# Score banks in two halves, an order for TensorE from a list scheduler, and the causal mask moved to GpSimd, in a two-stage attention kernel

## The chip, the cores and the metric

One core of one Trainium2 chip runs the kernel. The metric is the time of one execution in device microseconds; of a set of runs the median counts. The core has TensorE (PE; its loads of stationary operands are the row PEld), VectorE (DVE), ScalarE (ACT), GpSimd (POOL) and SyncE (SP), each working through its own instructions in order. The queues of DMA transfers that SP and GpSimd start run beside them. PSUM, into which TensorE writes, has eight banks of 512 f32 values for each of the 128 partitions.

## The reference

Two stages follow one another. Stage A is an attention over 8 batches of 12 heads, 448 positions and head size 64; stage B runs four attention experts over its result, of which each token uses two.

```
# stage A, for each batch and head
scores = cap * tanh(q @ k.T / 8 / cap);  attn = softmax(scores);  x[:, head] = attn @ v
# stage B, for each batch; x is 448 x 768
logits = x @ w_gate;  w = softmax over the two largest of four
for e in range(4):
    q, k, v = x @ wq[e], x @ wk[e], x @ wv[e]            # 448 x 64 each
    a = softmax(where(causal, -1e9, q @ k.T / 8));  out += w[e] * (a @ v @ wo[e])
```

The tanh keeps the scores within 30, so that stage A needs no maximum; each score is passed once through Tanh and once through Exp on ScalarE.

## The kernel before

Two heads make a pair: six pairs to a batch, 48 in all. The loop over `p` runs through the pairs, and stage B of a batch is spread over the eight passes behind its last pair, so that both stages share the engines. The order on every engine is the order in which the code issues the work (`manual_schedule`); a table, `batch_b`, says which unit of stage B is issued at which place of which pass.

A pair goes through these steps. `load` fetches the f32 inputs of a whole batch with seven DMAs from SP (the first batch in four groups). `a_cast` (GpSimd) makes f16 copies. `a_tr` (TensorE, then DVE) transposes q and k. `fill0` writes the transposed scores of head 0 and the tails of both heads, four blocks of 128 keys by 448 queries, into a tile of four PSUM banks, and `fill1` the three blocks of head 1. This tile, `ps_score`, exists once: a fill can only start when ScalarE has read the tile's last content, and ScalarE can only go on with scores when the fill is done. `tanh` reads a whole tile (1792 or 1344 values for each partition), `expo` makes the exponentials from its f16 result. `a_pv` multiplies by v, with a column of ones that gives the sum, into two more banks; `a_norm` divides. `a_xt` transposes back into `xT`, and its copy on DVE (L281) also brings the queries, which are held as c·112+p for query 4p+c, into their order with a strided write.

Stage B reads `xT`: `b_v`, `b_gate`, `b_q` and `b_k` project; `b_fill` writes the scores of two experts into the same four-bank tile, a mask being added to each diagonal block by a matmul of `ltm` (L383); `b_exp` takes the exponential of all 1984 columns at once; `b_pv1`, `b_ot` and `b_wo` finish, and the result leaves by DMA from SP. These units use two PSUM banks in turn, `ps_aux`. One pass issues

```
tanh(p,0)  fill1(p)  expo(p-1,1)  a_pv(p-1,0)  a_tr(p+2)  a_cast(p+3)  units of B  tanh(p,1)
fill0(p+1)  expo(p,0)  a_pv(p-1,1)  a_norm(p-1)  units of B  a_xt(p-1)
```

and in two passes of a batch `b_fill` and `b_exp` take the tile between `tanh(p,1)` and `fill0(p+1)`, with `expo(p,0)` cut in two around them.

## Time and profile before

| | |
|---|---|
| Median of 3 runs | 443.25 us (442.03 to 443.75) |
| Profiled execution | 441.75 us, of which its span on the engines 440.0 us |
| Busy: PE, PEld, DVE, ACT, POOL | 311.9, 205.7, 276.6, 305.7, 132.8 us |
| First tanh starts, last expo of stage A ends | 11.66 us, 401.65 us |
| Mean granted clock of TensorE | 0.939 of 2.4 GHz |
| HBM read and written | 36.19 MB, 11.01 MB |

Busy time is the union of an engine's instructions. Two that follow one another closely overlap in the records, so the step from one start to the next is what a chain costs. A busy TensorE is not one at its peak, since a matmul's record also holds the time in which it drains.

### The profile page before, as it was taken

The page shows a single profiled execution, that of the slowest core. Times are in us where ns is not written, and L with a number is a line of the kernel's source. Part 1 is how long each engine was busy: PE and PEld are TensorE (multiplying, and loading weights), DVE is VectorE, ACT ScalarE, POOL GpSimd, SP SyncE. Part 2 cuts the span into 40 slices and gives each one's busy share as a digit, 9 for nine tenths or more (in the row PEclk, how much of TensorE's full clock was granted, in tenths as well). Part 3 has the DMA queues.
Part 4 walks back from the last instruction along what each step waited for, and adds up shares of the span by engine and source line. Part 5 has one row for each costly group of instructions (what it writes and reads, how often), then busy time and mean ns, then how long its engine had stood idle before and what let it go on. Part 6 is the DMA issues. An engine that isn't in the chain of part 4 may idle for free.

```text
span 440.0 us, 8813 instructions
## 1 busy us (share of the span) xinstructions
PE 311.9 (71%) x3568; PEld 205.7 (47%) x3568; DVE 276.6 (63%) x693; ACT 305.7 (69%) x231; POOL 132.8 (30%) x374
## 2 busy tenths in 40 slices
PE   2676686857759677667868587686776678686865
PEld 1354464545535454444536454355544455354442
DVE  6145476567836588468755678365884687557745
ACT  1779797987757777788758877578767887584030
POOL 6793973233223323223322332233232220000000
PEclk9999899899977999999997999779999999979896
DMA  5999998001191012900184012910110001000303
GB/s 139 282 238 229 247 266 253 2 2 72 59 324 51 1 73 80 336 17 37 74 251 144 1 73 65 332 35 2 72 55 3 1 36 72 19 1 9 118 1 125
DMA packets 63497, 46.19 MB, mean 105 GB/s; under 512 B 24288, under 2 KB 59872, under 8 KB 63456
## 3 DMA queue, kind: packets, MB, share of 16 engines
q1 hardware_dynamic: 52944, 44.05, 34.3%
q0 software_dynamic: 10512, 1.58, 4.8%
q8 instruction: 28, 0.46, 0.5%
q14 instruction: 13, 0.11, 0.1%
HBM read 36.19 MB, written 11.01 MB: 107 GB/s over the span
## 4 chain that ended last, share of the span: by engine, by line
PE 45%; DVE 29%; ACT 10%; SPq 6%; issue 5%; DMA 3%; POOL 1%; DVEq 0%; ACTq 0%; POOLq 0%
PE pv L245 8%; PE s L191 6%; ACT pB L389 6%; DVE ob L443 5%; PE kps L357 4%; PE s L202 4%; DVE xT L281 4%; DVE xk L257 4%; PE vps L300 3%; PE sB L378 3%; PE qps L347 3%; PE xtp L270 2%; PE wops L438 2%; DVE kzB L361 2%; DVE kz L180 2%
## 5 line engine op out<-in xcount | busy, mean ns | idle before, releaser
L215 ACT ACTIVATE y<-s 128x1792 f16<-128x1792 f32 x96 | 141.8, 1477 | 53.6 <-PE s L195 33.5
L226 ACT ACTIVATE p<-y 128x1792 f16<-128x1792 f16 (+2 forms) x110 | 147.2, 1339 | 0.0
L136 POOL CAST q<-qf 112x512 f16<-112x512 f32 x48 | 29.5, 614 | 205.1 <-PE tps L164 176.8
L245 PEld LDWEIGHTS <-p 128*128 128x128 f16 x1536 | 66.6, 103 | 21.8 <-issue 6.2
L245 PE MATMUL pv<-v,p 128*128 128x65 f16 x1152 | 66.2, 201 | 0.8 <-ACT p L226 0.8
L281 DVE COPY xT<-xtp 128x448 f16<-128x448 f16 x48 | 55.9, 1164 | 11.4 <-PE xtp L270 11.1
L389 ACT ACTIVATE pB<-sB 128x1984 f16<-128x1984 f32 x16 | 29.2, 1824 | 46.2 <-PE sB L383 46.2
L191 PE MATMUL s<-qt,kz 128*128 128x448 f16 x144 | 40.7, 397 | 27.1 <-ACT pB L389 24.9
L245 PE MATMUL pv<-vtz,p 128*128 128x65 f16 x384 | 58.8, 199 | 0.0
L255 DVE RECIPROCAL rc<-pv 128x8 f32<-128x8 f32 x48 | 10.0, 208 | 75.6 <-PE pv L245 75.6
L438 PE MATMUL wops<-wo,oT 128*128 128x384 f16 x128 | 32.2, 348 | 18.2 <-DVE kz L180 10.3
L177 DVE COPY qt<-tps 128x576 f16<-128x576 f16 x48 | 22.3, 465 | 33.8 <-PE tps L171 33.7
L202 PE MATMUL s<-qt,kz 128*128 128x448 f16 x144 | 39.7, 389 | 4.9 <-ACT y L215 4.8
L443 DVE COPY ob<-wops 128x384 f32<-128x384 f32 (+1 forms) x64 | 34.6, 557 | 5.6 <-PE wops L438 4.6
L257 DVE TENSOR_TENSOR xk<-pv,rc 128x512 f16<-128x512 f32 x48 | 33.2, 692 | 1.7
L270 PE MATMUL xtp<-ident,xk 128*128 128x128 f16 x144 | 17.2, 232 | 23.4 <-DVE xk L257 20.6
L191 PEld LDWEIGHTS <-kz 128*128 128x128 f16 x144 | 14.7, 106 | 38.8 <-issue 32.9
L164 PE MATMUL tps<-ident,q 112*128 112x112 f16 x192 | 19.1, 227 | 13.2 <-POOL q L136 9.3
L270 PEld LDWEIGHTS <-xk 128*128 128x128 f16 x192 | 12.6, 102 | 33.9 <-DVE xk L257 25.9
L347 PE MATMUL qps<-xT,wq 128*128 128x448 f16 x96 | 23.3, 384 | 5.9 <-DVE ob L443 5.8
L300 PE MATMUL vps<-wvg,xT 128*128 128x260 f16 x192 | 26.5, 283 | 1.0
L146 POOL CAST v<-vf 128x384 f16<-128x384 f32 x48 | 24.4, 507 | 8.9 <-DMA vf<-in_v_dram 6.2
(86 smaller groups left out, 510.9 us busy)
## 6 DMA issues: line engine op xcount, KB each, us to landing
qf<-in_q_dram SPq DMA_DIRECT2D x7, 1344.0 KB, 8.5
out_dram<-ob SPq DMA_DIRECT2D x24, 384.0 KB, 2.3
kf<-in_k_dram SPq DMA_DIRECT2D x7, 1152.0 KB, 10.8
vf<-in_v_dram SPq DMA_DIRECT2D x7, 1152.0 KB, 8.3
out_dram<-ob SPq DMA_DIRECT2D x8, 192.0 KB, 2.7
ktf<-in_k_dram SPq DMA_DIRECT2D x14, 96.0 KB, 9.4
vtf<-in_v_dram SPq DMA_DIRECT2D x14, 96.0 KB, 6.8
qf<-in_q_dram SPq DMA_DIRECT2D x2, 448.0 KB, 5.1
```

Source lines behind the costliest of these rows:

```text
L191: nc.tensor.matmul(sc[:, c, 0:S], kk[:, 0, 128 * c : 128 * (c + 1)], qt[:, 0:S], start=True, stop=True,)
L202: nc.tensor.matmul(sc[:, c, 0:S], kk[:, 1, 128 * c : 128 * (c + 1)], qt[:, 0:S], start=True, stop=True,)
L215: nc.scalar.activation(yt, sc[:, 0:n, 0:S], AF.Tanh, scale=isc / capf)
L226: nc.scalar.activation(pt[:, c0:c1, :], yt[:, c0:c1, :], AF.Exp, scale=capf)
L245: nc.tensor.matmul(pv[:, g, 65 * n : 65 * n + 65], lhsT, rhs, start=(c == 0), stop=(c == KC),)
L257: nc.vector.tensor_tensor(xk.rearrange("p n g d -> p g n d"), pv[:, :, :, 0:64], rc.broadcast_to((128, 2, 4, Dh)), ALU.mult,)
L270: nc.tensor.transpose(ps[:, 128 * n : 128 * (n + 1)], src(n), ident if n < 3 else swap)
L281: nc.vector.tensor_copy(xT[b][:, j, :].rearrange("m (p c) -> m c p", c=QC), ps[:, 0:S].rearrange("m (c p) -> m c p", c=QC),)
L300: nc.tensor.matmul(ps, xT[b][:, j, WIN[n] : WIN[n] + 128], wvg[:, j, :], start=(j == 0), stop=(j == NDC - 1))
L389: nc.scalar.activation(pb[:, 64:2048], s.pop(("sc", r))[:, 0:1984], AF.Exp, scale=isc)
L438: nc.tensor.matmul(ps, s["oT"][r][:, w : w + 128], wo2[r][:, f * (D // 2) : (f + 1) * (D // 2)], start=(r == 0), stop=(r == 1),)
L443: nc.vector.tensor_copy(ob[lo:128, f * (D // 2) : (f + 1) * (D // 2)], ps[lo:128, :])
```

## The change

The score tile becomes two tiles of two banks each. A pair's seven blocks go through them in four parts (`HALF`: 2, 2, 2 and 1 blocks), each part with a `fill` and a `tanh` of its own, and the two tiles are refilled in turn: while ScalarE reads one, TensorE may write the other. `expo` stays one instruction for four and one for three blocks. Stage B's scores go the same way, one expert (1024 or 960 columns) for each half tile. ScalarE's order is written down as a list, `prog`: for each pair two tanhs, the exponential of the head before, two tanhs, the exponential of head 0, with stage B's exponentials (`X`) in two passes of a batch.

TensorE's order is no longer a table. A class `Plan` keeps estimated clocks of TensorE, DVE and ScalarE while the program is built. Before each fill it issues the units that can start before the half tile comes free (`pump`), and holds back those that would end too late for the fill; it forces what the fill depends on. Stage B's units of a batch carry earliest times spread over 36 us. Nothing of this runs on the chip; it only sets the order of the instructions.

The causal mask is taken off TensorE: instead of adding -30000 before the exponential, GpSimd sets the masked values to zero after it, with eight `affine_select`s for each two experts. The fills read the queries in another order, with a strided moving operand, as a block of 384 columns and one of 64, so that each window of 128 columns holds 128 successive queries; the transposes of `a_xt` then bring them into order by a permuted identity, and the copy to `xT` becomes contiguous. `a_pv` has a bank of its own for each head and divides at once, so that reciprocal and product come once for each head; there are four auxiliary banks for it and all other units. Loads come pair by pair, seven ahead; casts run four ahead. Before the first transposes fourteen matmuls on zeros are issued, and pair 0 is cast by DVE.

```diff
+class Plan:
...
+    LAT = 0.2
...
+    def emit(self, u):
+        start = max(self.pe, self.ready(u))
+        u["fn"]()
+        self.pe = start + u["pe"]
+        end = self.pe + self.LAT
+        if u["dve"]:
+            self.dve = max(self.dve, end) + u["dve"]
+            end = self.dve + self.LAT
+        if u["aux"]:
+            self.aux[self.naux % 4] = end
+            self.naux += 1
+        self.done[u["key"]] = end
...
+    def pump(self, until, latest):
+        while self.pe < until and (self.work or self.paced):
+            best = None
+            for q in (self.work, self.paced[:1]):
+                for u in q:
+                    r = self.ready(u)
+                    if r is not None and (best is None or max(r, self.pe) < best[0]):
+                        best = (max(r, self.pe), u)
+            if best is None or best[0] > until or best[0] + best[1]["pe"] > latest:
+                return
+            u = best[1]
+            (self.work if u in self.work else self.paced).remove(u)
+            self.emit(u)
...
-    stage = ctx.enter_context(tc.tile_pool(name="stage", bufs=2))
+    stage = ctx.enter_context(tc.tile_pool(name="stage", bufs=8))
...
+    def load(p):
...
+        nc.sync.dma_start(qf, q[b, h0:h1].rearrange("h (p c) d -> p h (c d)", c=QC))
+        nc.sync.dma_start(kf, k[b, h0:h1, 0:KM].rearrange("h (p c) d -> p h (c d)", c=KC))
...
+        staged[p] = (qf, kf, vf, ktf, vtf)
...
+    LOAD, CAST, TR = 7, 4, 2
+    for p in range(4):
+        load(p)
...
+    HALF = (((0, 0), (0, 1)), ((0, 2), (0, 3)), ((1, 0), (1, 1)), ((1, 2),))
...
+    def fill(p, i):
...
+        sc = ps_score.tile([128, 2, 512], f32, name=f"s{i}_{p}", tag="score")
+        m = qt[:, 0:S].rearrange("m (c p) -> m c p", c=QC)
+        main = m[:, :, 0:96].rearrange("m c (n t) -> m n c t", t=32)
+        tail = m[:, :, 96:QP]
+        for o, (g, c) in enumerate(HALF[i]):
+            lhsT = qt[:, S : S + 128] if c == KC else kk[:, g, 128 * c : 128 * (c + 1)]
             nc.tensor.matmul(
-                sc[:, c, 0:S], kk[:, 0, 128 * c : 128 * (c + 1)], qt[:, 0:S],
-                start=True, stop=True,
-            )
-        nc.tensor.matmul(sc[:, 3, 0:S], qt[:, S : S + 128], qt[:, 0:S], start=True, stop=True)
-        score[(p, 0)] = sc
-    def fill1(p):
-        qt, kk = qkt.pop(p)
-        sc = ps_score.tile([128, 4, 512], f32, name=f"s1_{p}", tag="score")
-        for c in range(KC):
+                sc[:, o, 0:KM].rearrange("m (n c t) -> m n c t", n=3, c=QC),
+                lhsT, main, start=True, stop=True,
+            )
             nc.tensor.matmul(
-                sc[:, c, 0:S], kk[:, 1, 128 * c : 128 * (c + 1)], qt[:, 0:S],
-                start=True, stop=True,
-            )
-        score[(p, 1)] = sc
+                sc[:, o, KM:S].rearrange("m (c t) -> m c t", c=QC),
+                lhsT, tail, start=True, stop=True,
+            )
+        score[(p, i)] = sc
...
+    def tanh(p, i):
+        g = i // 2
+        n = len(HALF[i])
+        if i % 2 == 0:
+            y[(p, g)] = actp.tile([128, 4 - g, S], f16, name=f"y{g}_{p}", tag=f"y{g}")
+        nc.scalar.activation(
+            y[(p, g)][:, 2 * (i % 2) : 2 * (i % 2) + n, :], score.pop((p, i))[:, 0:n, 0:S],
+            AF.Tanh, scale=isc / capf,
+        )
+    def expo(p, g):
+        pt = actp.tile([128, 4 - g, S], f16, name=f"p{g}_{p}", tag=f"p{g}")
+        nc.scalar.activation(pt, y.pop((p, g)), AF.Exp, scale=capf)
+        pr[(p, g)] = pt
...
+        pv = ps_aux.tile([128, 4, Dh + 1], f32, name=f"pv{g}_{p}", tag="aux")
...
+                nc.tensor.matmul(pv[:, n, :], lhsT, rhs, start=(c == 0), stop=(c == KC))
...
+        nc.vector.reciprocal(rc, pv[:, :, Dh : Dh + 1])
         nc.vector.tensor_tensor(
-            xk.rearrange("p n g d -> p g n d"),
-            pv[:, :, :, 0:64],
-            rc.broadcast_to((128, 2, 4, Dh)),
-            ALU.mult,
+            xt[p][:, :, g, :], pv[:, :, 0:Dh], rc.broadcast_to((128, 4, Dh)), ALU.mult
         )
-        xt[p] = xk
...
-        transpose4(ps, lambda n: xk[:, n, :, :].rearrange("p g d -> p (g d)"))
-        nc.vector.tensor_copy(
-            xT[b][:, j, :].rearrange("m (p c) -> m c p", c=QC),
-            ps[:, 0:S].rearrange("m (c p) -> m c p", c=QC),
-        )
+        transpose4(ps, lambda n: xk[:, n, :, :].rearrange("p g d -> p (g d)"), perm, pswap)
+        nc.vector.tensor_copy(xT[b][:, j, :], ps[:, 0:S])
...
+    def b_fill(b, r, g):
...
+        sc = ps_score.tile([128, 1024], f32, name=f"sB{g}_{b}_{r}", tag="score")
+        if g == 0:
+            nc.tensor.matmul(sc[:, 0:64], kk[:, KM : KM + 128], qe[:, KM:S], start=True, stop=True)
+        for (e, c), o in COL.items():
+            if e == g:
+                n = S - 128 * c
+                o -= 1024 * g
+                ko = e * (S + TL) + 128 * c
+                nc.tensor.matmul(
+                    sc[:, o : o + n], kk[:, ko : ko + 128], qe[:, 128 * c : S],
+                    start=True, stop=True,
+                )
+        s["sc", r, g] = sc
...
+    def b_exp(b, r, g):
...
+        pb = pB[2 * (b % 2) + r]
+        n = 1024 - 64 * g
+        o0 = 64 + 1024 * g
+        nc.scalar.activation(
+            pb[:, o0 : o0 + n], st[b].pop(("sc", r, g))[:, 0:n], AF.Exp, scale=isc
         )
+        blocks = [(o, 0, 128, 128) for (e, _), o in COL.items() if e == g]
+        if g == 0:
+            blocks += [(0, 0, 64, 64), (0, 64, 128, 64)]
+        for o, r0, r1, n in blocks:
+            blk = pb[r0:r1, 64 + o : 64 + o + n]
+            nc.gpsimd.affine_select(
+                out=blk, in_=blk, compare_op=ALU.is_ge, fill=0.0, base=0,
+                pattern=[[1, n]], channel_multiplier=-1,
+            )
...
+    dummy = ps_aux.tile([128, 512], f32, name="dummy", tag="aux")
+    for _ in range(14):
+        nc.tensor.matmul(dummy, warm[:, 0:128], warm, start=True, stop=True)
...
+    a_cast(0, nc.vector)
+    a_tr(0)
     a_cast(1)
...
+    nc.vector.tensor_copy(
+        perm.rearrange("r (p c) -> r c p", c=QC), ident.rearrange("r (c p) -> r c p", c=QC)
+    )
...
+    prog = []
+    for p in range(NP + HP):
+        ops = []
+        if p < NP:
+            ops += [("S", p), ("T", p, 0), ("T", p, 1)]
+        else:
+            ops += [("S", p)]
+        xb = EXPB.get(p)
+        if xb:
+            ops.append(("X", *xb, 0))
+        if 1 <= p <= NP:
+            ops.append(("E", p - 1, 1))
+        if xb:
+            ops.append(("X", *xb, 1))
+        if p < NP:
+            ops += [("T", p, 2), ("T", p, 3), ("E", p, 0)]
+        prog += ops
...
+    def do_fill():
+        nonlocal nfill
+        o = reads[nfill]
+        rel = ends[nfill - 2] if nfill >= 2 else 0.0
+        cost = 0.43 if o[0] == "X" else 0.38 if o[2] < 3 else 0.19
+        dep = fill_dep(o)
+        plan.force(dep)
+        at = plan.act + sum(dur(x) for x in prog[pos : where[nfill]])
+        plan.pump(rel, at - cost - 0.4)
+        plan.pe = max(plan.pe, rel, plan.done[dep]) + cost
+        fill(*o[1:]) if o[0] == "T" else b_fill(*o[1:])
...
+    def slot(p):
+        load(p + LOAD)
+        if CAST <= p + CAST < NP:
+            a_cast(p + CAST)
+            plan.done[("cast", p + CAST)] = plan.act + 4.0
+        if p < 4:
+            weights(p)
+        if p + TR < NP:
+            plan.add(work, ("tr", p + TR), 0.43, 0.95, [("cast", p + TR)], a_tr, p + TR)
+        if p >= 1 and p <= NP:
+            plan.add(work, ("pv", p - 1, 0), 0.73, 0.55, [("E", p - 1, 0)], a_pv, p - 1, 0)
+            plan.add(
+                work, ("pv", p - 1, 1), 0.73, 0.55, [("E", p - 1, 1), ("pv", p - 1, 0)],
+                a_pv, p - 1, 1,
+            )
+            plan.add(work, ("xt", p - 1), 0.22, 0.35, [("pv", p - 1, 1)], a_xt, p - 1)
+        if p >= HP and p % HP == 0:
+            batch(p // HP - 1)
...
+    def batch(b):
...
+        for r in range(2):
+            plan.add(u, ("q", b, r), 1.13, 0.55, [x], b_q, b, r)
+            plan.add(u, ("k", b, r), 1.13, 0.75, [x], b_k, b, r)
+            for n in range(2 * r, 2 * r + 2):
+                plan.add(u, ("v", b, n), 0.66, 0.6, [x], b_v, b, n)
+        plan.add(u, ("g", b), 0.0, 1.4, [("v", b, 3)], b_gates, b, aux=False)
+        for e in range(E):
+            plan.add(
+                u, ("pvB", b, e), 0.46, 0.7, [("X", b, e // 2, e % 2), ("g", b)], b_pv, b, e
+            )
+            if e % 2:
+                plan.add(u, ("oT", b, e // 2), 0.22, 0.35, [("pvB", b, e)], b_ot, b, e // 2)
+        for n in range(4):
+            for f in range(2):
+                plan.add(u, ("wo", b, n, f), 0.33, 0.5, [("oT", b, 1)], b_wo, b, n, f)
+        if b < B - 1:
+            for i, t in enumerate(u):
+                t["nb"] = plan.act + 4.0 + i * 36.0 / len(u)
+        paced.extend(u)
```

## Rows read from the trace of the kernel before

**Rows 1.** Waits, by who waited for whom: total us, times, longest us.
```profile
ACT pB L389 <- PE sB L383: 46.2, 16, 5.7
...
ACT y L215 <- PE s L195: 33.5, 34, 9.6
...
ACT y L215 <- PE s L202: 19.8, 20, 1.4
```

**Rows 2.** Windows, by batch: length, busy PE PEld DVE ACT POOL (count), clock, DMA.
```profile
11.66:50.80 39.14, 25.96 (x255) 16.55 (x255) 14.71 (x30) 32.74 (x23) 28.73 (x63) 0.97 1.31 250
...
94.76:147.80 53.04, 39.07 (x452) 25.91 (x449) 34.00 (x84) 38.22 (x30) 14.56 (x43) 0.90 0.34 105
...
301.40:350.45 49.05, 35.20 (x452) 23.88 (x449) 34.02 (x84) 38.02 (x30) 14.56 (x43) 1.00 0.08 30
...
401.65:440.00 38.35, 25.56 (x187) 13.85 (x184) 23.61 (x66) 3.87 (x4) 0.00 (x0) 0.84 0.20 73
```

**Rows 3.** Timeline of ACT in a stretch without waits: start, us, instruction.
```profile
34.43 1.28 ACT L215 ACTIVATE y<-s 128x1344 f16<-128x1344 f32 x1
35.60 1.70 ACT L226 ACTIVATE p<-y 128x1792 f16<-128x1792 f16 x1
37.19 1.66 ACT L215 ACTIVATE y<-s 128x1792 f16<-128x1792 f32 x1
38.73 1.33 ACT L226 ACTIVATE p<-y 128x1344 f16<-128x1344 f16 x1
39.94 1.30 ACT L215 ACTIVATE y<-s 128x1344 f16<-128x1344 f32 x1
```

**Rows 4.** Timeline of ACT, the first tanh and one exponential of stage B.
```profile
11.66 1.66 ACT L215 ACTIVATE y<-s 128x1792 f16<-128x1792 f32 x1 [9.64 <-PE s L195]
...
75.61 1.82 ACT L389 ACTIVATE pB<-sB 128x1984 f16<-128x1984 f32 x1 [3.10 <-PE sB L383]
```

**Rows 5.** Timeline of PE: one dense stretch, and one fill elsewhere.
```profile
103.89 0.73 PE L202 MATMUL s<-qt,kz 128*128 128x448 f16 x3
104.46 0.26 PE L245 MATMUL pv<-v,p 128*128 128x65 f16 x3
...
104.96 0.36 PE L164 MATMUL tps<-ident,q 112*128 112x112 f16 x4
...
105.38 0.33 PE L438 MATMUL wops<-wo,oT 128*128 128x384 f16 x1
...
127.87 1.28 PE L191 MATMUL s<-qt,kz 128*128 128x448 f16 x3 [1.91 <-ACT pB L389]
```

**Rows 6.** Lines of DVE by shape: count, busy us, mean ns, idle before.
```profile
L281 DVE COPY xT<-xtp 128x448 f16<-128x448 f16 x48 | 55.9, 1164 | 11.4 <-PE xtp L270 11.1
...
L257 DVE TENSOR_TENSOR xk<-pv,rc 128x512 f16<-128x512 f32 x48 | 33.2, 692 | 1.7
...
L443 DVE COPY ob<-wops 128x384 f32<-128x384 f32 x48 | 26.1, 556 | 5.4 <-PE wops L438 4.6
...
L255 DVE RECIPROCAL rc<-pv 128x8 f32<-128x8 f32 x48 | 10.0, 208 | 75.6 <-PE pv L245 75.6
...
L417 DVE TENSOR_TENSOR osc<-pvB,sl 128x256 f16<-128x256 f32 x32 | 13.6, 425 | 1.1
...
L427 DVE COPY oT<-otp 128x448 f16<-128x448 f16 x16 | 5.5, 382 | 0.4 <-PE otp L270 0.4
```

**Rows 7.** Lines by shape of other engines.
```profile
L383 PE MATMUL sB<-ident,ltm 128*128 128x128 f16 x96 | 17.6, 219 | 0.0
...
L322 ACT ACTIVATE eexp<-lg 128x16 f32<-128x16 f32 x8 | 1.8, 219 | 21.1 <-DVE lg L311 21.1
...
masks.py:66 POOL TENSOR_SCALAR_AFFINE_SELECT ltm<-ltm 128x128 f16<-128x128 f16 x1 | 0.3, 295 | 0.1
```

**Rows 8.** Timeline of SP, one load's issue.
```profile
9.95 0.66 SPq L82 DMA_DIRECT2D ktf<-in_k_dram  x1
```

**Rows 9.** Timeline of DVE, its last instructions.
```profile
433.97 2.31 DVE L443 COPY ob<-wops 128x384 f32<-128x384 f32 x4 [0.25 <-PE wops L438]
```

More of the change, by code (lines that the diff above doesn't have):

```diff
@@ new lines, in load @@
+        staged[p] = (qf, kf, vf, ktf, vtf)
+    LOAD, CAST, TR = 7, 4, 2
+    for p in range(4):
+        load(p)
+    warm = const.tile([128, 512], f16, name="warm")
+    nc.vector.memset(warm, 0.0)
+    ident = const.tile([128, 128], f16, name="ident")
+    make_identity(nc, ident)
+    kz = [const.tile([128, 2, KM], f16, name=f"kz{i}") for i in range(4)]
+    ktz = [const.tile([128, 128], f16, name=f"ktz{i}") for i in range(6)]
+    for t in kz + ktz:
+        nc.vector.memset(t, 0.0)
+    cast = {}
@@ new lines, in a_cast @@
+    def a_cast(p, eng=None):
+        if p >= NP:
+            return
+        eng = nc.gpsimd if eng is None else eng
+        assert p < 8 or ("pv", p - 8, 1) in plan.done and ("tr", p - 6) in plan.done
+        qf, kf, vf, ktf, vtf = staged.pop(p)
+        q16 = hd.tile([QP, QC, 2, Dh], f16, name=f"q16_{p}", tag="q16", bufs=6)
+        k16 = hd.tile([128, KC, 2, Dh], f16, name=f"k16_{p}", tag="k16", bufs=6)
+        eng.tensor_copy(q16, qf.rearrange("p h (c d) -> p c h d", c=QC))
+        eng.tensor_copy(k16, kf.rearrange("p h (c d) -> p c h d", c=KC))
+        for g in range(2):
+            r = slice(64 * g, 64 * (g + 1))
+            eng.tensor_copy(ktz[p % 6][r, r], ktf[r, :])
@@ L400, in b_pv1 @@
             w = WIN[n]
[L401 removed]
             ops = []
[L403 to L405 removed]
+            for c in range(KC):
+                if 128 * c <= w:
+                    ops.append((64 + COL[(g, c)] + w - 128 * c, s["vall"][:, c, e, :]))
             if n == 3:
@@ new lines @@
+    work, paced = plan.work, plan.paced
+    EXPB = {HP * (b + 1) + 3 + 2 * r: (b, r) for b in range(B) for r in range(2)}
+    prog = []
[3 more added lines that the diff above has]
+            ops += [("S", p), ("T", p, 0), ("T", p, 1)]
+        else:
+            ops += [("S", p)]
[9 more added lines that the diff above has]
+        prog += ops
@@ new lines, with dur, fill_dep @@
+    reads = [o for o in prog if o[0] in "TX"]
+    where = [i for i, o in enumerate(prog) if o[0] in "TX"]
+    ends = {}
+    nfill = 0
+    pos = 0
+    def dur(o):
+        if o[0] == "S":
+            return 0.0
+        if o[0] == "X":
+            return 0.9
+        return 0.06 + 0.373 * (4 - o[2] if o[0] == "E" else len(HALF[o[2]]))
+    def fill_dep(o):
+        return ("tr", o[1]) if o[0] == "T" else ("k", o[1], o[2])
+    def do_fill():
[9 more added lines that the diff above has]
+        fill(*o[1:]) if o[0] == "T" else b_fill(*o[1:])
+        plan.done[("f", nfill)] = plan.pe + plan.LAT
+        nfill += 1
@@ new lines, in b_gates @@
+    def b_gates(b):
+        b_gexp(b)
+        plan.act += 0.1
+        b_gate(b)
+    a_cast(2)
+    a_cast(3)
+    for p in range(4):
+        plan.done[("cast", p)] = 0.0
+    for p in range(4, LOAD):
+        load(p)
+    plan.done[("tr", 0)] = 0.0
+    a_tr(1)
+    plan.done[("tr", 1)] = 0.0
+    do_fill()
+    do_fill()
+    nread = 0
+    for pos, o in enumerate(prog, 1):
+        if o[0] == "S":
+            slot(o[1])
+            continue
+        if o[0] == "E":
+            plan.act += dur(o)
+            expo(*o[1:])
+            plan.done[o] = plan.act + plan.LAT
+            continue
+        while nfill <= nread:
+            do_fill()
+        start = max(plan.act, plan.done[("f", nread)])
+        if o[0] == "T":
+            tanh(*o[1:])
+        else:
+            b_exp(*o[1:])
+            plan.done[o] = start + dur(o) + plan.LAT + 1.2
+        plan.act = start + dur(o)
+        ends[nread] = plan.act
+        nread += 1
+        while nfill < len(reads) and nfill - 2 in ends and plan.known(fill_dep(reads[nfill])):
+            do_fill()
```

394 lines of the change are left out of this document (133 added, 261 removed).

## The prediction, made before the change was run

> **What bounds the kernel now.** I read the waits first. ScalarE waits for TensorE's scores in three places: 33.5 us before four-block tanhs, 19.8 before three-block ones, 46.2 before stage B's exponentials [rows 1]. Together 99.5 us; 9.6 is the start [rows 4]. The cause is in the code: one score tile, so that a fill waits for ScalarE's read and the next read for the fill. Where ScalarE has something else to do meanwhile (the exponential of the other head), the fill hides; where TensorE has units of stage B standing before the fill, or where `b_fill` takes the tile, it does not.
>
> The windows then show where. The first batch, with no stage B beside it, takes 39.1 us; later ones 49 to 53, with every engine's busy time far below: PE 35.2, DVE 34.0, ACT 38.0 of 49.05 [rows 2]. So none of them is the bound there; the order of handing the tile over is. The stretch from 34 to 40 us shows what ScalarE can do with its data ready: its steps from start to start are 1.17, 1.59, 1.54 and 1.21 us, 5.51 for a pair [rows 3]. After the last exponential of stage A 38.35 us remain, a chain in which DVE is busy 23.6 and PE 25.6 [rows 2]. I therefore sum four terms: start, first batch, seven batches with stage B beside them, tail. In the profiled execution they are 11.7, 39.1, 350.85 and 38.35, its span of 440.0.
>
> **The parts of the change, ScalarE's own time.** A tanh of 1792 values steps 1.54, one of 1344 1.17 [rows 3]: 0.37 for a block of 448 and 0.06 for the instruction. Two tanhs more a pair cost 0.12, so 5.63. What the trace lacks is a tanh directly behind a tanh, which comes twice a pair: its step is at least the one above, and at most the whole duration, 1.66 for 4 blocks or 0.18 for the instruction, 0.12 more [rows 3]. I take 0.05 each, the nearer end being the exponential that follows a tanh at full overlap: 5.73 a pair, bounds 5.63 and 5.87.
>
> Stage B's exponential of 1984 columns lasts 1.82 [rows 4]; its step is shorter by the overlap and splitting adds 0.06, so 1.82 for two halves, 3.64 a batch. The gate's small one adds at most 0.22 [rows 7]. A batch of six pairs then costs ScalarE 34.4 + 3.6 + 0.2 = 38.2, against the 49 to 53 it takes now.
>
> **Whether the fills keep up.** In a pair ScalarE reads tanh 0, tanh 1, exponential, tanh 2, tanh 3, exponential. A half tile freed by tanh 0 is read again by tanh 2, with tanh 1 (0.80) and an exponential (1.21) between; the fill must fit into 2.0. Three blocks of fill take 0.57 from start to start (103.89 to 104.46) [rows 5], so 0.19 a block and some 0.4 a half with its tails. That leaves 1.4 for whatever unit of TensorE is running, and the longest (six matmuls of 448 columns in `b_q`) is 1.14. Stage B's halves have less: the first stands right behind tanh 0 and tanh 1, so only tanh 1's 0.8 covers a fill of 0.43. If TensorE is free this hides; if a long unit stands there, up to 1.1 is lost, four times a batch. I take 0.3 each, 1.2 a batch, since the planner holds long units back before a fill; bounds 0 and 4.4. A batch comes to 39.4.
>
> **TensorE's load.** Full-clock steps: a fill block 0.19, the sixteen matmuls of `a_pv` 0.50 (104.46 to 104.96), the eight transposes of `a_tr` 0.42 [rows 5], so 0.05 a transpose and 0.03 a 65-column matmul. Splitting a block of 448 into 384 and 64 gives 0.16 + 0.03: nothing. That the moving operand is strided shows nowhere in this trace; bounds: no cost, or half rate, 0.16 more a block. I take none, the nearest row being today's fill, which reads the same values in another order; half rate is a rival below. A pair is 7 x 0.19 + 2 x 0.50 + 0.42 + 4 x 0.05 = 2.95. Stage B: 24 matmuls in `b_q` and `b_k` 4.6, 24 of 260 columns in `b_v` 2.7, 16 of 384 in `b_wo` 2.6, 40 in `b_pv` 1.2, 8 transposes 0.4, scores of 3968 columns 1.7: 13.2. The mask's matmuls (12 of 128 columns a batch by their count of 96, and two of 64) [rows 7] go away, 0.7 saved. A batch is 6 x 2.95 + 13.2 = 30.9 of 39.4, at the full clock: TensorE has a fifth to spare. Half clock would end that; the same three matmuls have lasted 1.28 instead of 0.73 after a wait of 1.9 us for ScalarE [rows 5].
>
> **DVE, GpSimd, SP.** The copy to `xT` takes 1164 ns; the same shape written contiguously, `oT`, takes 382 [rows 6]. Six a batch save 4.7. The product split by heads costs 2 x 425 instead of 692, and a second reciprocal at most its 208 [rows 6]: 2.2 more. DVE falls from 34.0 to about 31.5 of 39.4, cover enough for the four auxiliary banks, two of which were tied to `pv` before. Sixteen selects a batch at 295 ns [rows 7] take GpSimd from 14.6 [rows 2] to 19.3. They stand between an exponential and `b_pv`, up to five in a row, 1.5 us, and behind a pair's casts; what waits is `b_pv`, which has the rest of the batch as cover. If that cover is gone, as in the tail, they cost their 1.5. Loads: seven issues a pair, at most 0.66 each [rows 8], 4.6 of SP's 5.7; they run seven pairs ahead into eight buffers, so that they wait for nothing recent, and an output that waits on SP for DVE delays loads with some three pairs of slack. I cost them at nothing.
>
> **Start.** The first tanh now waits for four blocks, then for two. At the half clock a block takes 0.18 more than at the full one ((1.28 - 0.73)/3 [rows 5]), 0.37; two blocks less, 0.7. The first casts and loads stay as early; GpSimd's 32 small memsets and DVE's cast of pair 0 shift against each other. I take 11.0, bounds 10 and 13.
>
> **Tail.** What is in it now: 17.5 us of DVE once batch 6's rest is taken out (eight copies of 0.556, two of 0.382, two products of 0.425: 6.1 of 23.6) [rows 2, 6]. Its idle time there is 14.7, of which some 3 at the front (pv, division, transposes, q) and 3.7 behind the last copy, 436.3 to 440 [rows 9]. With all idle kept 32.2, with only front and end 24.2. The gate, k's copies and the order q, k, v of the list still make TensorE wait, so I take 30.
>
> **Sum.** First batch: 34.4 and 0.5 for the filling of the loop, 34.9. 11.0 + 34.9 + 7 x 39.4 + 30 = 351.7. The profiled execution had 1.75 outside its span, and the median of the runs lies 1.5 above it: 351.7 + 3.25 = **355**. Differences under 0.5% I count as no change, about what a measurement of this kernel can tell.
>
> **The rivals.** *TensorE's order still stands in the way*: each unit waits in order for DVE, GpSimd or a bank, and what is planned in estimated clocks drifts from the chip's. Of ScalarE's 99.5 us of waits 80 lie between start and tail (less 9.6, and about 9.4 in the tail), ten for each of the eight batches. If half stays, a batch is 38.2 + 5 = 43.2, the sum 378.3 and 3.25 more: 382. For it: three engines at 78 to 97% of 39.4. Against it: the loads above, and two half tiles.
>
> *Half rate of the strided fills*: 42 blocks x 0.16 = 6.7 more, TensorE 37.6 of 39.4; with waits between units some 44 a batch: 11 + 34.9 + 308 + 30 + 3.25 = 387. For it speaks only that no row excludes it; against it, that the values lie in runs of 32.
>
> *Slower, by the clock*: many short fills, each waiting for ScalarE, keep TensorE at 1.2 GHz. Its 30.9 a batch become 62, and 11 + 36 + 7 x 62 + 40 + 3.25 = 524, with the first batch at its own half-clock work and a tail as long as now. It decides from 50.1 a batch, where the sum reaches 441, that is when some six tenths of the batch's work run at the half clock (30.9 x 1.62). Against it: the windows at 1.00 with PE busy 35.2 of 49 and 0.97 with 26.0 of 39.1 [rows 2]; low stretches, as 0.90 in the batch of 53.04 us, come with long waits. The Trainium skill's "TensorE: Matmul & The Clock Gate" (A second HAM failure mode: psum-queue depth-cycling) speaks for this rival: it tells of a kernel that cycles its PSUM banks and idles so often between groups of matmuls that the clock goes up and down. By that rule the sum could reach 524; by the windows, in which the kernel already idles between groups at 1.00, it is not likely.
>
> *Faster still*: no wait left, 5.63 a pair, 37.6 a batch, tail 25: 10.5 + 34.3 + 263.2 + 25 + 3.25 = 336.
>
> **Chances.** 355, with a range of its own from 340 to 368: 0.60. Faster still: 0.10. TensorE's order: 0.20. Half rate: 0.05. Clock: 0.05. The range 338 to 390 leaves out some 0.08 below and 0.10 above. Of the clock case nearly all is slower; so faster 0.93, same 0.02, slower 0.05.
>
> **What would show it.** Right: ScalarE's waits for scores fall from 99.5 to under 30 us; a batch takes 38 to 41 us; tanh steps of 0.80 and 0.43; the copy to `xT` near 380 ns; a clock near 1.00 from pair 2 on. Wrong: waits of ScalarE that stay above 50 (TensorE's order; TensorE would then wait for DVE, GpSimd or ScalarE right ahead of fills), 384-column matmuls that step 0.3 instead of 0.16 (strided reads), a clock under 0.8 in the batches, a tail still at 38.

## The result and the profile after

The changed kernel takes 356.73 us (355.87 to 358.11, median of 4 runs) against 443.31 (442.03 to 443.75, 4 runs) before: a ratio of 0.8054, 95% interval 0.8019 to 0.8089. 355 was forecast. The profiled execution has a span of 355.7 us. The lines below are windows of the trace after, cut as in [rows 2]: the start, the first batch, a batch nearly without waits, one with a wait of 2.30 us, the tail. The columns are length, busy PE, PEld, DVE, ACT and POOL (count), clock, DMA share, GB/s.

```profile
0.00:11.08 11.08, 7.69 (x35) 3.56 (x36) 7.19 (x28) 1.28 (x1) 7.83 (x48) 0.92 0.51 144
11.08:47.49 36.41, 25.14 (x316) 17.48 (x314) 15.50 (x53) 32.83 (x35) 28.70 (x63) 0.84 1.11 189
...
120.96:158.97 38.01, 33.83 (x451) 24.21 (x448) 28.23 (x84) 37.81 (x43) 18.45 (x60) 1.00 0.53 153
197.02:237.13 40.11, 34.74 (x477) 25.01 (x476) 32.06 (x101) 37.81 (x43) 18.37 (x60) 1.00 0.52 151
...
318.23:355.70 37.47, 23.62 (x188) 13.85 (x186) 23.20 (x67) 3.99 (x5) 4.12 (x17) 0.82 0.21 75
```

A batch of 53.0 or 49.05 us has become one of 37.5 to 38.05, or of 40.1 where ScalarE waits; in that of 38.01 ScalarE is busy for 37.8. The seven periods, from the exponential of pair 5's head 0 to that of pair 11 and so on, are 37.59, 37.46, 38.01, 38.05, 40.11, 38.05 and 40.12. Against the four terms of the forecast:

| us | forecast | measured |
|---|---|---|
| Start, to the first tanh | 11.0 | 11.08 |
| First batch, to pair 6's first tanh | 34.9 | 36.41 |
| Seven batches | 275.8 | 270.74 |
| Tail, from the end of the last `expo` | 30 | 37.47 |
| Sum, the span | 351.7 | 355.7 |

The waits of ScalarE, as in [rows 1] (total, times, longest), fell from 99.5 to 35.3 us:

```profile
ACT pB L418 <- PE sB L406: 22.7, 9, 13.4
ACT y L258 <- PE s L244: 12.6, 3, 9.0
```

Of these 9.0 are the start and 13.4 + 3.7 lie in the tail. Nearly all of the rest are four waits in the timeline of ACT (start, us, instruction, idle before it): 2.39 (shown) and 1.19 in the first batch, and 2.30 in each of the two batches of 40.1 us. Five waits of 0.2 at stage B's scores make up what is left.

```profile
15.20 1.35 ACT L258 ACTIVATE y<-s 128x896 f16<-128x896 f32 x2 [2.39 <-PE s L244]
16.43 1.70 ACT L265 ACTIVATE p<-y 128x1792 f16<-128x1792 f16 x1
18.02 1.73 ACT L258 ACTIVATE y<-s 128x896 f16<-128x896 f32 x2
19.61 1.34 ACT L265 ACTIVATE p<-y 128x1344 f16<-128x1344 f16 x1
20.83 1.37 ACT L258 ACTIVATE y<-s 128x896 f16<-128x896 f32 x2
22.05 1.73 ACT L265 ACTIVATE p<-y 128x1792 f16<-128x1792 f16 x1
...
219.70 1.02 ACT L418 ACTIVATE pB<-sB 128x1024 f16<-128x1024 f32 x1 [2.30 <-PE sB L406]
220.62 1.32 ACT L265 ACTIVATE p<-y 128x1344 f16<-128x1344 f16 x1
221.84 0.96 ACT L418 ACTIVATE pB<-sB 128x960 f16<-128x960 f32 x1
```

The first two tanhs of a pair take 1.59 (18.02 to 19.61), the exponential of three blocks 1.22, the other two tanhs 1.22, the exponential of four blocks 1.59 (16.43 to 18.02): 5.6 for a pair.

What TensorE does ahead of the wait at 219.70 is the reading on which most experiments turn. Its timeline in that stretch:

```profile
214.63 1.14 PE L479 MATMUL wops<-wo,oT 128*128 128x384 f16 x6
215.61 1.30 PE L371 MATMUL qps<-xT,wq 128*128 128x448 f16 x6
216.74 1.30 PE L381 MATMUL kps<-xT,wk 128*128 128x448 f16 x6
219.00 0.20 PE L400 MATMUL sB<-qe,kzB 128*128 128x64 f16 x1 [0.95 <-DVE kzB L387]
219.03 1.02 PE L406 MATMUL sB<-qe,kzB 128*128 128x448 f16 x6
```

The output matmuls of the batch before, the queries and the keys come all in one block, and the scores then wait for the copies of the keys. One batch earlier the queries went out at 174.56 and the keys at 176.48, with other work between, and ScalarE waited 0.19. Stage B is late in the list here, and is caught up at the last moment by `force`, which issues what the next fill depends on with all that stands ahead of it in its queue.

### The profile page after: what moved, and what is told of

Its sections match the earlier page's. It is cut to its first block, busy times and chain, and to the rows that moved or that the text cites. A ratio compares the mean times of both kernels' runs of the same rounds, so it can differ in the third digit from the quotient of the medians.

```text
span 355.7 us, 10216 instructions
## 1 busy us (share of the span) xinstructions
PE 292.0 (82%) x3806; PEld 206.5 (58%) x3806; DVE 253.6 (71%) x800; ACT 303.3 (85%) x329; POOL 162.7 (46%) x523
## 4 chain that ended last, share of the span: by engine, by line
ACT 60%; PE 22%; DVE 6%; SPq 5%; issue 2%; POOL 2%; DMA 1%; DVEq 0%; POOLq 0%; ACTq 0%
ACT p L265 28%; ACT y L258 27%; ACT pB L418 5%; PE s L240 4%; PE wops L479 4%; PE kps L381 3%; PE qps L371 3%; PE pv L280 2%; PE sB L406 2%; DVE kzB L386 2%; PE vps L321 2%; SPq L153 1%; DMA ktf<-in_k_dram 1%; SPq L156 1%; DVE osc L456 1%
## 5 line engine op out<-in xcount | busy, mean ns | idle before, releaser
L258 ACT ACTIVATE y<-s 128x896 f16<-128x896 f32 x192 | 154.3, 892 | 12.6 <-PE s L244 12.6
L265 ACT ACTIVATE p<-y 128x1792 f16<-128x1792 f16 x96 | 151.0, 1574 | 0.0
L426 POOL TENSOR_SCALAR_AFFINE_SELECT pB<-pB 128x128 f16<-128x128 f16 (+1 forms) x128 | 31.7, 278 | 154.3 <-ACT pB L418 153.1
L240 PE MATMUL s<-qt,kz 128*128 128x384 f16 x288 | 77.7, 332 | 12.3 <-ACT y L258 5.1
L244 PE MATMUL s<-qt,kz 128*128 128x64 f16 x288 | 55.8, 194 | 0.0
L418 ACT ACTIVATE pB<-sB 128x1024 f16<-128x1024 f32 (+1 forms) x32 | 31.8, 1001 | 22.7 <-PE sB L406 22.7
L287 DVE TENSOR_TENSOR xk<-pv,rc 128x256 f16<-128x256 f32 x96 | 40.8, 424 | 3.3
L244 PEld LDWEIGHTS <-kz 128*128 128x128 f16 x288 | 28.2, 98 | 22.2 <-issue 19.9
L240 PEld LDWEIGHTS <-kz 128*128 128x128 f16 x288 | 28.5, 99 | 12.9 <-issue 1.4
L286 DVE RECIPROCAL rc<-pv 128x4 f32<-128x4 f32 x96 | 17.1, 178 | 18.0 <-PE pv L280 16.9
L194 POOL CAST vtz<-vtf 64x64 f16<-64x64 f32 x96 | 22.5, 234 | 5.0 <-DMA vtf<-in_v_dram 2.1
L185 POOL CAST k<-kf 128x384 f16<-128x384 f32 x47 | 23.8, 506 | 0.0
```

What stands on the lines that cost most here:

```text
L240: nc.tensor.matmul(sc[:, o, 0:KM].rearrange("m (n c t) -> m n c t", n=3, c=QC), lhsT, main, start=True, stop=True,)
L244: nc.tensor.matmul(sc[:, o, KM:S].rearrange("m (c t) -> m c t", c=QC), lhsT, tail, start=True, stop=True,)
L258: nc.scalar.activation(y[(p, g)][:, 2 * (i % 2) : 2 * (i % 2) + n, :], score.pop((p, i))[:, 0:n, 0:S], AF.Tanh, scale=isc / capf,)
L265: nc.scalar.activation(pt, y.pop((p, g)), AF.Exp, scale=capf)
L287: nc.vector.tensor_tensor(xt[p][:, :, g, :], pv[:, :, 0:Dh], rc.broadcast_to((128, 4, Dh)), ALU.mult)
L418: nc.scalar.activation(pb[:, o0 : o0 + n], st[b].pop(("sc", r, g))[:, 0:n], AF.Exp, scale=isc)
```

## The experiments

Each run is compared with the kernel before, which took 442.9 to 443.4 us beside them; the ratios are to it. Differences between two changed kernels are those of their medians, and under 3 us they are little more than the spread of the runs. Where a run changes the work of a unit, the planner's price for it is changed too.

**One half tile instead of two.** `e1_one_half`:

```diff
-tc.tile_pool(name="ps_score", bufs=2, space=bass.MemoryType.PSUM)
+tc.tile_pool(name="ps_score", bufs=1, space=bass.MemoryType.PSUM)
...
-rel = ends[nfill - 2] if nfill >= 2 else 0.0
+rel = ends[nfill - 1] if nfill >= 1 else 0.0
...
```

> One half tile instead of two; each fill waits for the tanh just ahead of it, and the planner is told so. Theory (the two halves let ScalarE run without waits): in each pair the second and the fourth tanh stand right behind another tanh, so that a fill of two blocks (some 0.6 us with its drain and hand-over) and one of one block (0.45) lie bare, 1.05 us a pair or 50 us; the exponentials of stage B add some 1.3 us each time, 18 us. Together 415 to 430 us. Rival (the list scheduler, the copy to xT and the mask made the gain, the halves are a detail): under 375 us.

Measured: 500.82 us, ratio 1.1307 (1.125 to 1.1364), slower even than before; batches of 53 to 58. Its waits, the largest group of TensorE's and ScalarE's two:

```profile
PE s L240 <- ACT y L258: 103.8, 116, 1.6
ACT pB L418 <- PE sB L406: 84.8, 18, 18.7
ACT y L258 <- PE s L244: 78.9, 112, 8.6
```

With one tile two of a pair's four fills are handed over bare, 0.63 and 0.44 us a time in a stretch at the full clock, and each of the two engines takes turns in waiting for the other. Two rows of ACT's timeline, and one of TensorE's:

```profile
207.59 0.54 ACT L258 ACTIVATE y<-s 128x448 f16<-128x448 f32 x1 [0.44 <-PE s L244]
...
211.15 0.92 ACT L258 ACTIVATE y<-s 128x896 f16<-128x896 f32 x1 [0.63 <-PE s L244]
```

```profile
244.42 3.02 PE L479 MATMUL wops<-wo,oT 128*128 128x384 f16 x16
```

That would be 6.4 us a batch; some waits are longer (1.54 at 204.21), and a steady batch has 8.8 in all. Two waits for stage B's scores, 2.97 and 5.97, come on top, 84.8 in the whole run where 18 had been expected. They are not in the main the price of the hand-over: ahead of the wait of 5.97 TensorE issues sixteen output matmuls, the queries and the keys in one block, as in the kernel after, and more of them. What the second half tile itself takes away is the other group, ScalarE's waits ahead of its tanhs: 70.3 us here without the start, 3.6 after. So without it the list gains nothing, and some 67 us of ScalarE's waits hang on it. How the list would do with the one four-bank tile of the kernel before, or two halves with that kernel's table, no run shows.

**More work on ScalarE.** `e4_more_act` repeats the exponential of one block in each pair, into a tile that nobody reads:

```diff
...
+        if g == 0:
+            again = actp.tile([128, S], f16, name=f"again_{p}", tag="again")
+            nc.scalar.activation(again, yt[:, 0, :], AF.Exp, scale=capf)
```

> ScalarE takes the exponential of one block of each pair a second time, into a tile that nobody reads: 0.43 us from start to start, 48 times. Theory (ScalarE sets the time between first tanh and last exponential): all of it shows, 20.6 us, 375 to 380 us. Rival (TensorE's order or DVE set the time, ScalarE is busy only because waits are hidden in its records): less than half of it shows, 357 to 367 us.

Measured: 368.34 us, 0.8311 (0.8294 to 0.8328), 11.6 above after. The repeated exponential steps 0.46:

```profile
100.85 0.68 ACT L269 ACTIVATE again<-y 128x448 f16<-128x448 f16 x1
101.31 1.82 ACT L258 ACTIVATE y<-s 128x896 f16<-128x896 f32 x2
```

The seven periods are 40.25 to 40.73, and the five that have no wait of 2.30 in after have grown by 2.3 to 2.9; six steps are 2.8. So ScalarE's steps set the batch. The total falls short of 48 steps, 22 us, because the two waits in the batches of 40.1 are gone, the first tanh comes 0.6 earlier, the waits of the first batch take up 1.0 of its 2.8, and the tail is 3.5 shorter; slack elsewhere was filled.

**The planner without its guard.** `pump` holds a unit back if it would end too late for the next fill. `e7_no_latest` drops that:

```diff
-        plan.pump(rel, at - cost - 0.4)
+        plan.pump(rel, 1.0e9)
```

> The planner no longer holds back units that would end too late for the next fill. Theory (fills are covered by two instructions of ScalarE; only stage B's fills are covered by one): waits of up to 1.1 us at the four fills of stage B in a batch, and some at the others; 0.5 to 3 us a batch, 360 to 378 us. Rival (TensorE's order doesn't matter within the slack): within 2 us of 356.7.

Measured: 349.95 us, 0.7893 (0.7866 to 0.7919), 6.8 faster than after. My theory was the reverse of what happens: the guard doesn't prevent waits, it makes them. The units held back are forced later, all together. Without it no batch is over 37.99, and in the profiled runs the time from the first tanh to stage A's last exponential is 4.5 us shorter and the tail 3.1 (34.4 instead of 37.5). The keys go out well before the scores need them; TensorE's timeline, half a pair long:

```profile
181.28 0.73 PE L371 MATMUL qps<-xT,wq 128*128 128x448 f16 x3
181.84 0.33 PE L240 MATMUL s<-qt,kz 128*128 128x384 f16 x1
...
183.18 1.30 PE L381 MATMUL kps<-xT,wk 128*128 128x448 f16 x6
184.31 0.33 PE L240 MATMUL s<-qt,kz 128*128 128x384 f16 x1
```

A fill stands directly behind the six matmuls of the keys and ScalarE doesn't wait: the other half tile covers it.

**The mask back on TensorE**, with the guard (`e2_mask_on_pe`) and without (`e9_mask_on_pe_no_latest`):

```diff
+            nc.tensor.matmul(sc[:, 0:64], ltm2, ident[:, 0:64], start=False, stop=True)
...
+                nc.tensor.matmul(sc[:, o : o + 128], ltm, ident, start=False, stop=True)
...
-            nc.gpsimd.affine_select(
-                out=blk, in_=blk, compare_op=ALU.is_ge, fill=0.0, base=0,
-                pattern=[[1, n]], channel_multiplier=-1,
-            )
```

> The causal mask goes back to TensorE as matmuls ahead of the exponential; the selects of GpSimd are gone. Theory (ScalarE's own work sets the time, TensorE has a fifth to spare): the batches stay at 38.7 us but for up to 0.2 us at each of stage B's fills, and the tail loses the selects' 1 us: 354 to 361 us. Rival (taking the mask off TensorE was worth its 0.7 us a batch and shorter fills): each of the 28 fills in the loop shows 0.2 us more to ScalarE, 362 us or more.

> The mask on TensorE, with a planner that holds no units back; beside the 349.95 us of the kernel that only holds none back. Order theory (the mask's longer fills cost 11.7 us only by way of the holding back): 348 to 352 us. Rival (the mask's matmuls cost ScalarE time at each fill of stage B): 358 us or more.

Measured: 368.39 us (0.8311, 0.8299 to 0.8323) and 352.08 (0.795, 0.792 to 0.798). With the guard the edit costs 11.7: some 6.4 between the first tanh and the last exponential, where four of the seven batches have a wait of 2.44 to 3.02 at stage B's scores instead of two with 2.30, and 4.9 in the tail, which becomes 42.4. Without the guard the edit costs 2.1, at most a little more than the spread of the runs. So moving the mask is worth some 2 us by itself, and the rest is the list's order.

**The queries' order as before**: contiguous fills and the strided copy to `xT`, with the guard (`e3_query_order`) and without (`e10_query_order_no_latest`):

```diff
-            nc.tensor.matmul(
-                sc[:, o, 0:KM].rearrange("m (n c t) -> m n c t", n=3, c=QC),
-                lhsT, main, start=True, stop=True,
-            )
...
+            nc.tensor.matmul(sc[:, o, 0:S], lhsT, qt[:, 0:S], start=True, stop=True)
...
-        nc.vector.tensor_copy(xT[b][:, j, :], ps[:, 0:S])
+        nc.vector.tensor_copy(
+            xT[b][:, j, :].rearrange("m (p c) -> m c p", c=QC),
+            ps[:, 0:S].rearrange("m (c p) -> m c p", c=QC),
+        )
```

> The queries are read in their old order with one contiguous matmul a block, and the copy to xT writes with a stride again. TensorE has seven matmuls less a pair, DVE 0.78 us more a pair. Theory (ScalarE's own work sets the time): DVE goes from about 30 to 34.5 of 38.7 us a batch and still fits, 356 to 365 us, with 0.8 to 3 us of it in the tail and some waits on auxiliary banks. Rival (the copy was what held the loop, since DVE would be at nine tenths and TensorE waits for its banks): two to five us a batch, 372 to 395 us.

> The old order of the queries and the strided copy to xT, with a planner that holds no units back; beside 349.95 us. Order theory: DVE's 0.78 us more a pair still fits, some of it shows in the tail, 350 to 356 us. Rival (DVE's longer chain delays TensorE through the auxiliary banks): 362 us or more.

Measured: 370.88 us (0.8357, 0.8327 to 0.8387) and 367.53 (0.829, 0.8265 to 0.8315). The copy's cost isn't hidden: 14.2 above after, and 17.6 above the kernel without a guard. The second is in the range of the rival that was put against it. Without the guard DVE is busy 283.1 us in all, 251.6 with the contiguous copy. Batches of 40.7 have one wait of 2.74, and it is again the block of output matmuls, queries and keys; the timeline of TensorE without the guard:

```profile
177.09 0.54 PE L240 MATMUL s<-qt,kz 128*128 128x448 f16 x2 [0.55 <-ACT y L251]
...
178.35 1.14 PE L475 MATMUL wops<-wo,oT 128*128 128x384 f16 x6
179.32 1.30 PE L367 MATMUL qps<-xT,wq 128*128 128x448 f16 x6
180.46 1.30 PE L377 MATMUL kps<-xT,wk 128*128 128x448 f16 x6
182.71 0.20 PE L396 MATMUL sB<-qe,kzB 128*128 128x64 f16 x1 [0.95 <-DVE kzB L383]
```

One fill ahead of the block TensorE waits 0.55 for ScalarE: it is not late there, and the block stands in the list. Nor does the rival's mechanism show: in the batch from 142.7 to 183.4 TensorE's waits for DVE are 3.1 us, for the products and the keys that its matmuls read, and none of them is for an auxiliary bank. So the wait comes from the list's order, made with a dearer copy. Whether with better prices DVE, busy 34.8 of 40.7, would have had the room, no run tells. Without this part of the change dropping the guard is worth 3.4 us instead of 6.8.

**More work on TensorE.** Three kernels repeat the transposes of `a_tr` (those of the queries twice, those of the keys three times), writing the same values again: with the guard (`e6_more_pe`), without it (`e8_more_pe_no_latest`), and without it and with the planner's figure for `a_pv` set to the 0.50 us that the trace shows instead of 0.73 (`e12_true_cost`):

```diff
...
+            for _ in range(2):
...
+            for _ in range(3):
...
-        plan.pump(rel, at - cost - 0.4)
+        plan.pump(rel, 1.0e9)
...
-            plan.add(work, ("pv", p - 1, 0), 0.73, 0.55, [("E", p - 1, 0)], a_pv, p - 1, 0)
+            plan.add(work, ("pv", p - 1, 0), 0.50, 0.55, [("E", p - 1, 0)], a_pv, p - 1, 0)
...
```

> TensorE makes ten of its transposes of q and k a second time, writing the same values: about 0.52 us more a pair at the full clock, 3.1 us a batch, 25 us in all. The planner is told. Theory (TensorE has a fifth to spare): its load goes from some 31 to 34 of 38.7 us a batch and the time stays, 356 to 361 us. Rival (TensorE in its order is as much a bound as ScalarE): most of it shows, 370 to 382 us.

> The doubled transposes (0.52 us of TensorE a pair) together with a planner that holds no units back. Two theories of why the doubled transposes alone cost 27 us: order (the planner, with less room between fills, holds stage B's long units back until a fill of stage B forces them all at once; ScalarE stands for 5 us once a batch): without the holding back the batches return to about 38 us, 350 to 357 us. Capacity (TensorE's work has no room left): 370 us or more.

> As the kernel before this in the series (the doubled and tripled transposes of a_tr, no guard, 368.62 us), with one edit: the planner's figure for the unit a_pv is 0.50 instead of 0.73, the step from start to start that the trace shows (sixteen matmuls of 65 columns). Nothing else of the work differs; the repeated transposes write the same values again. Theory, an order from a clock that runs too fast: by its own figures TensorE has 6.3 us of work in a pair of 6.3, so that stage B's units are always behind, the output matmuls of the batch before, the queries and the keys come all at once ahead of stage B's first scores, and ScalarE waits 2.63 there once a batch. With 0.46 a pair less in that clock the wait goes and a batch falls from 40.7 to about 38: 348 to 356. Rival, TensorE itself is full (busy 37.0 of 40.7): the wait moves or stays, and the time is 364 to 370.

Measured: 383.47 us (0.8642, 0.8611 to 0.8674), 368.62 (0.8312, 0.8288 to 0.8336) and 352.17 (0.7946, 0.7896 to 0.7996). After the first two I held that TensorE had less room than forecast. The third refutes that: the three kernels have the same matmuls and differ by nothing but the order in which they are issued, and they are 33.5, 18.7 and 2.2 us above the kernel without a guard and without the repeats, 349.95. The 2.2 is no clean price of the work, since no run has the lower figure for `a_pv` without the repeats, and the intervals of the two overlap. Ahead of stage B's scores, the timeline of TensorE in the second (ScalarE then waits 2.63 at 186.13) and in the third (no wait):

```profile
180.73 1.46 PE L481 MATMUL wops<-wo,oT 128*128 128x384 f16 x8
182.03 1.30 PE L373 MATMUL qps<-xT,wq 128*128 128x448 f16 x6
183.17 1.30 PE L383 MATMUL kps<-xT,wk 128*128 128x448 f16 x6
```

```profile
176.81 1.30 PE L383 MATMUL kps<-xT,wk 128*128 128x448 f16 x6
```

In the third the scores follow the keys by 2.3 us, with transposes between (179.13). One batch of the first and one of the third, as windows of two kernels:

```profile
208.50:251.50 43.00, 37.80 (x537) 28.06 (x536) 30.19 (x97) 37.77 (x43) 18.28 (x60) 1.00 0.44 130
```

```profile
197.75:236.26 38.51, 36.25 (x539) 27.78 (x536) 30.26 (x97) 37.77 (x42) 18.36 (x60) 1.00 0.50 147
```

In 43.00 us ScalarE waits once, 5.04 us, for stage B's first scores. In 38.51 TensorE does the same work, and the largest wait is 0.49. The tail, too, shows how late the list is: 41.5, 38.1 and 33.6 us in the three. A planner that prices a unit too high believes TensorE full, lets the paced units slip, and pays at the point where they are forced. A whole-batch busy share of 37.8 of 43.0 looked like a full engine, and was not one.

**The tail's order.** In the last batch `e5_tail_order` puts the first eight units of stage B ahead of what is left of batch 6:

```diff
-        paced.extend(u)
+        if b < B - 1:
+            paced.extend(u)
+        else:
+            paced[:] = u[:8] + paced + u[8:]
```

> In the tail the first eight units of the last batch's stage B stand ahead of what is left of the batch before it. Theory (the tail did not shrink because the list forces sixteen output matmuls of the batch before ahead of the last pair's product with v, which starts 6 us after its exponential): the last pair's product starts within 1 us of its exponential, and the leftover goes into gaps behind; 3 to 6 us less, 350 to 354 us. Rival (the tail is set by the sum of DVE's copies, whatever their order): within 1 us of 356.7.

Measured: 361.14 us (0.8167, 0.8138 to 0.8196), 4.4 slower than after, which is outside both ranges. The front did get shorter: the first exponential of stage B in the tail starts 7.76 after stage A's last, instead of 13.37. But batch 6's rest then stood between the projections and the gate, on TensorE and on DVE, and the tail grew to 42.3. Here the leftover cost more behind the projections than in front of them.

**Together.** `e11_tail_and_start` drops the guard, takes stage B's exponentials a pair earlier and spreads its units over 30 us instead of 36, so that less is left over; in the last batch the queries and keys go first, and ScalarE makes some of DVE's copies; the casts of pairs 2 to 7 get later times in the plan.

```diff
-    EXPB = {HP * (b + 1) + 3 + 2 * r: (b, r) for b in range(B) for r in range(2)}
+    EXPB = {HP * (b + 1) + 2 + 2 * r: (b, r) for b in range(B) for r in range(2)}
...
-                t["nb"] = plan.act + 4.0 + i * 36.0 / len(u)
+                t["nb"] = plan.act + 3.0 + i * 30.0 / len(u)
...
+            paced[:0] = [last[k_] for k_ in first]
...
+        if b == B - 1 and f == 0:
+            nc.scalar.activation(ob[lo:128, c0:c1], ps[lo:128, :], AF.Copy)
...
```

> No units held back; stage B's exponentials one pair earlier in each batch, so that less of the batch before is left at the end; the last pair's product and the last batch's q and k ahead of what is left; in the last batch ScalarE makes the copies of q and half of the output's; the planner is told that the first casts come later. Theory (what is left are the tail, a chain of late units, and two waits in the first batch for casts that the planner thought done): first batch 1 to 3 us shorter, tail 26 to 29 instead of 34.4 us, 338 to 345 us. Rival (the tail is DVE's sum of copies): 347 us or more.

Measured: 347.63 us (0.7839, 0.7817 to 0.7862), the fastest of all; 9.1 below after and 2.3 below the guard's removal alone. Seven batches of 37.5 to 38.0, a tail of 32.2, a first tanh at 10.59. Of the first batch's two waits the first shrank to 0.17 and the second grew from 1.19 to 2.41. 338 to 345 had been expected, with the tail's gate to cost less: DVE's chain for it still keeps TensorE idle for 3.45 us. The time lies just inside the range given to the rival, a tail set by the sum of DVE's copies; the run does not part the two.

## Why the prediction was right, and where it was not

**The main mechanism held.** Handing over one score tile was the bound, and two halves remove it: with one of them some 67 us of ScalarE's waits ahead of its tanhs come back. ScalarE's waits came to 35.3 where under 30 was named; 17.1 of them lie in the tail. ScalarE is the bound of the batches: 37.5 by its own steps, the two periods without a wait, and shown by the run with more of its work.

**The batches, 39.4 forecast, 38.7 measured.** Two items were too high. A tanh directly behind a tanh costs nothing extra (0.05 each was taken, some 0.6 a batch): two of them step 1.59 against 0.80 twice. Waits at stage B's fills were put at 1.2 a batch; they are 0 to 0.4 in five and 2.30 in two, 0.8 on average. Their cause was not the one named, a long unit standing by chance in front of a fill, but stage B running late in the list; and the guard, which the forecast counted on to keep them small, is what makes them: without it the waits of 2.30 are gone.

**The first batch, 34.9 forecast, 36.4 measured.** I gave 0.5 for the filling of the loop; two waits of 2.39 and 1.19 came. The timelines of GpSimd and of TensorE ahead of the first:

```profile
12.22 0.61 POOL L184 CAST q<-qf 112x512 f16<-112x512 f32 x1 [1.33 <-DMA qf<-in_q_dram]
```

```profile
12.89 0.56 PE L204 MATMUL tps<-ident,q 112*128 112x112 f16 x4 [1.10 <-POOL q L184]
13.81 0.29 PE L209 MATMUL tps<-ident,ktz 128*128 128x128 f16 x1 [0.36 <-POOL ktz L188]
...
14.21 0.52 PE L240 MATMUL s<-qt,kz 128*128 128x384 f16 x1
```

The list put `a_tr(2)` ahead of a fill that ScalarE was about to need; the transposes wait for GpSimd's cast, and that for its data. The fill waits behind both. I had costed loads and casts at nothing. TensorE's granted clock is 0.64 from 11.08 to 23, so that the late fill is a slow one as well. The clock of 1.00 "from pair 2 on" also fails for one stretch: it is 0.67 from 28.3 to 33.4 us, just ahead of the second of these waits.

**The tail is the step that failed: 30 forecast, 37.5 measured.** I had taken batch 6's rest, 6.1 us of DVE, out of the tail. It is still there, and it stands in front. TensorE's timeline, the first rows after stage A's last exponential ends at 318.23, and then DVE's:

```profile
319.42 0.50 PE L296 MATMUL otp<-ident,osc 128*128 128x128 f16 x3 [1.14 <-DVE osc L456]
...
320.52 4.02 PE L479 MATMUL wops<-wo,oT 128*128 128x384 f16 x15 [0.17 <-DVE oT L466]
324.38 0.33 PE L296 MATMUL xtp<-perm,xk 128*128 128x128 f16 x3
...
324.68 0.26 PE L280 MATMUL pv<-v,p 128*128 128x65 f16 x3
...
327.50 1.30 PE L371 MATMUL qps<-xT,wq 128*128 128x448 f16 x6
```

```profile
321.06 4.64 DVE L482 COPY ob<-wops 128x384 f32<-128x384 f32 x8 [0.60 <-PE wops L479]
...
341.59 0.17 DVE L364 TENSOR_TENSOR wtok<-wun,rden 128x16 f32<-128x16 f32 x1
```

The products of pair 47 need no more than that exponential, and start 6.4 us after it; the queries start at 327.50, 9.3 after it. In the forecast's own terms: its 30 were 17.5 us of DVE's work and 12.5 of its idle time. DVE was busy for 23.2 and idle for 14.3. So 5.7 of the 7.5 missed are the leftover that had been taken out, and 1.8 are idle time; that part was nearly right, with the gate's chain on DVE (to 341.76) and eight copies at the end. The tail is 37.5 where it was 38.35 before, near the 38 that the forecast named as a sign of being wrong. What failed was the assumption that a planner with all units listed would clear the batch before. Its paced queue is read from the head only, so the leftover goes first. One other order, that of the tail's experiment, was worse; dropping the guard, which leaves less over, gives 34.4.

**TensorE's room, "a fifth to spare".** True of the engine, as the run with a measured price for `a_pv` shows: 0.52 us a pair more, and ScalarE still sets a batch of 38.5. It was not true of the schedule, where the same work cost 26.7 us above after. The rival of TensorE's order was judged right in kind: what waits remain in the batches are the order's. Its size, 5 us a batch, was not reached.

**The other steps.** The copy to `xT` takes 389 ns, 382 were taken. Splitting and striding the fills costs TensorE nothing; half rate is out. A row of DVE's lines (count, busy us, mean ns) and four of TensorE's timeline:

```profile
L307 DVE COPY xT<-xtp 128x448 f16<-128x448 f16 x48 | 18.7, 389 | 3.8 <-PE xtp L296 2.8
```

```profile
121.00 0.33 PE L240 MATMUL s<-qt,kz 128*128 128x384 f16 x1
121.16 0.19 PE L244 MATMUL s<-qt,kz 128*128 128x64 f16 x1
121.19 0.33 PE L240 MATMUL s<-qt,kz 128*128 128x384 f16 x1
121.35 0.19 PE L244 MATMUL s<-qt,kz 128*128 128x64 f16 x1
```

A step of 0.16 and 0.03, 0.19 a block, as [rows 5] for a contiguous one. The clock rival is out: 1.00 in the batches. The Trainium skill's "TensorE: Matmul & The Clock Gate" (A second HAM failure mode: psum-queue depth-cycling) tells of a clock that goes up and down when banks are cycled with short idle times between groups; here two halves are cycled with TensorE busy 33.8 of 38.0, and the trace of the batches does not agree.

**How the errors stood to each other.** First batch 1.5 too low, batches 5.1 too high, tail 7.5 too low: 4.0 in the span. The median then lies 1.0 above the span where 3.25 had been added, which takes back 2.2. That 355 came so near 356.7 is in part luck, this cancelling. Left open is whether DVE has room for the strided copy in a better order than the one that cost 17.6 us, and what the tail could reach if batch 6's rest were cleared in time. The bank for each head's products, the two more auxiliary banks, the loads pair by pair and the fourteen matmuls at the start were never taken out one at a time, so their shares are not known.

## What to carry to other kernels

When a bound is the handing over of one buffer, a second half-size buffer can be worth more than a saving of work (some 67 us of ScalarE's waits hung on it here; moving the mask gave some 2 us), and the floor after it is the reader's own start-to-start steps. In a list made by a scheduler, price units by measured steps: a price too high (0.73 for 0.50, 16.5 us here) makes the plan believe an engine full, and the slipped units are paid for all at once at the point where something needs them; a single wait per period at one instruction, with a block of forced units ahead of it, is the sign. For a tail, list what the loop leaves over before counting what the tail must do.

## What the runs showed of the hardware

A moving operand read in runs of 32 f16 values (16 in the block of 64 columns) from four places costs TensorE nothing over a contiguous one: 0.19 us for 448 columns either way, at a clock of 1.00. DVE's copy of 128x448 f16 from PSUM takes 389 ns written contiguously and 1164 written with a stride [rows 6]. GpSimd's selects, 292 ns each for 128x128, stay off the path in the batches: the kernel without them is not faster. And where one tile is passed between TensorE and ScalarE with nothing to cover it, the hand-over with a fill of four matmuls is 0.63 us of ScalarE's time, at a clock of 1.00.
